# Spreading inverse softmax sums with a transpose and a constant selector

## The chip, the cores and the metric

The kernel runs on one core of a Trainium2 chip. The metric is the device time of one execution in microseconds (us); the time before is the median of three runs. TensorE is called PE here (PEld is its loading of weights), VectorE DVE, ScalarE ACT, GpSimd POOL, SyncE SP.

## The reference

Three layers follow each other, with batch 4, 8 heads, 576 tokens, head dimension 64:

```python
scores = scale * np.matmul(q, k.transpose(0, 1, 3, 2))
kth = np.partition(scores, -top_k, axis=-1)[..., -top_k:-top_k + 1]     # top_k = 32
scores = np.where(scores >= kth, scores, -1000000000.0)
attn = np.exp(scores - np.max(scores, axis=-1, keepdims=True))
attn = attn / (np.sum(attn, axis=-1, keepdims=True) + 1e-09)
out = np.matmul(attn, v)
...
x = sigmoid(xr @ w_r) * (np.maximum(xk @ w_k, 0) ** 2 @ w_v)            # xk, xr: token mixes of out
...
h = gelu(x @ w_in); u, v = halves of h; y = x + (u * (w_sg @ norm(v) + b_sg)) @ w_out
```

The change touches the division by the sum, and nothing else.

## The kernel before

The attention is worked off in 32 **units**: a batch, a pair of heads and a chunk of query tokens (`ch` 0 has 256 tokens, `ch` 1 has 320). In the first batch all chunks 0 come ahead of all chunks 1, later the two alternate. A unit is made of slots of 128 tokens (two for `ch` 0; two and a rest of 64 for `ch` 1, where both heads share the partitions). For each slot PE computes the scores (line 238), ACT copies them out of PSUM (240), DVE searches the 32nd largest score of each row by rounds of MAX8 (282) and MATCH_REPLACE8 (292) over the pairwise maxima and minima (273, 274), ACT takes the exponential (304), and DVE masks it and sums each row in one instruction (309). PE then transposes the masked rows (324, 327) and ACT copies them out (325, 328).

At the end of a unit `emit_unit` runs. DVE adds 1e-9 to the sums and inverts them (`rinv`, lines 345 and 346: 128 tokens on the partitions, 4 or 5 columns, one for each slot and head). PE multiplies the transposed probabilities by the values into the PSUM tile `px` (350, and 361 for the last 64 keys), with the head dimension on the partitions and the tokens along the free axis. The inverse sums have to stand in that layout too, so PE spreads each column of `rinv` over 64 partitions: the column, broadcast to 64 weights, times the identity (356, and 363 for the rest), both in full float32, into the PSUM tile `ps`. ACT copies `ps` to `rb` (366), and DVE multiplies `px` by `rb` into `x` (373, 377), from which the dense layers read.

PSUM has one double-bank for scores (tag `S`), three banks with the tag `tp` (the transposes of lines 198 to 216 and 324 to 336, and `px` and `ps`), and three with the tag `d` (dense layers). A `tp` bank is taken in the order in which the program asks for it and is free again when its last reader is done.

The dense layers of one batch (lines 522, 587, 607, 632, 713, 741) are put between the slots of the following attention work, by quotas of estimated PE time and by priorities; those of the last batch come after the last unit. A scheduler then sets the order of each engine's instructions from dependencies and priorities; on the chip each engine works its own list in that order.

Of the kernel before, what the change touches and what calls it, by code (L numbers as in the profile page):

```python
# [9 lines left out]
F32 = mybir.dt.float32  # L10
F32R = mybir.dt.float32r
I32 = mybir.dt.int32
U32 = mybir.dt.uint32
AF = mybir.ActivationFunctionType
OP = mybir.AluOpType
# [8 lines left out]
def computation(ctx, tc, dram, wscr, flag, fast, q, k, v, mu_k, mu_r, w_k, w_v, w_r, w_in, g_ln, w_sg, b_sg, w_out, out):  # L24
    nc = tc.nc
# [10 lines left out]
    const = ctx.enter_context(tc.tile_pool(name="const", bufs=1))  # L36
    sb = ctx.enter_context(tc.tile_pool(name="sb", bufs=1))
# [6 lines left out]
    ident = const.tile([128, 128], F32, name="ident")  # L44
# [5 lines left out]
    qrems = [const.tile([128, 2, 3, D], F32R, name=f"qrem{i}") for i in range(2)]  # L50
    for t in qrems:
        nc.vector.tensor_scalar(t[:, :, 1, :], ident[:, None, 0:64].to_broadcast([128, 2, D]), 0.0, None, op0=OP.mult)
    mu = const.tile([128, 2, KC], F32, name="mu")
    omu = const.tile([128, 2, KC], F32, name="omu")
    gln = const.tile([128, KC], F32, name="gln")
# [26 lines left out]
    def bank(tag, shape=(128, 512), dt=F32):  # L82
        if tag == "d" and rows[0] == NROWS:
            tag = ("d", "tp")[turn[0] % 2]
            turn[0] += 1
        return psum.tile(list(shape), dt, tag=tag, name=tag, bufs=BUFS[tag])
# [22 lines left out]
    for b in range(B):  # L109
# [4 lines left out]
        for p, chs in order:  # L114
            su = Rec()
            su.b, su.p, su.chs, su.raw, su.slots = b, p, chs, {}, []
            for ch in chs:
                u = Rec()
# [221 lines left out]
    def emit_unit(u):  # L340

        b, p, n, vr = u.su.b, u.su.p, u.n, u.su.raw["v"]
        nt = 4 if u.ch == 0 else 5
        rinv = sb.tile([128, 5], F32, tag="rinv", name="rinv", bufs=2)
        nc.vector.tensor_scalar(rinv[:, :nt], u.sums[:, :nt], 1e-9, None, op0=OP.add)
        nc.vector.reciprocal(rinv[:, :nt], rinv[:, :nt])
        px = bank("tp")
        for kc in range(4):
            for h in range(2):
                nc.tensor.matmul(px[64 * h:64 * h + 64, :n], lhsT=vr[:, 4 * h + kc, :], rhs=u.PT[h][:, kc, :n],  # L350
                                 start=(kc == 0), stop=False)

        ps = bank("tp")
        for i in range(2):
            for h in range(2):
                nc.tensor.matmul(ps[64 * h:64 * h + 64, 128 * i:128 * i + 128],
                                 lhsT=rinv[:, 2 * i + h:2 * i + h + 1].to_broadcast([128, 64]), rhs=ident,
                                 start=True, stop=True)
        for h in range(2):
            s = slice(64 * h, 64 * h + 64)  # L360
            nc.tensor.matmul(px[s, :n], lhsT=vr[s, 8, :], rhs=u.PTr[s, :n], start=False, stop=True)
            if u.ch:
                nc.tensor.matmul(ps[s, 256:320], lhsT=rinv[s, 4:5].to_broadcast([64, 64]), rhs=ident[s, s],
                                 start=True, stop=True)
        rb = sb.tile([128, 320], F32, tag="rb", name="rb", bufs=1)
        nc.scalar.activation(rb[:, :n], ps[:, :n], AF.Copy)
        if (b, p) not in xT:
            x = sb.tile([128, S + 1], F32, tag="x", name="x", bufs=5)
            xT[b, p] = x
            nc.gpsimd.memset(x[:, 0:1], 0.0)  # L370
        x = xT[b, p]
        o = 1 + 256 * u.ch
        nc.vector.tensor_tensor(x[:, o:o + 256].rearrange("p (i j) -> p j i", j=2),
                                px[:, :256].rearrange("p (j i) -> p j i", j=2),
                                rb[:, :256].rearrange("p (j i) -> p j i", j=2), op=OP.mult)
        if u.ch:
            nc.vector.tensor_tensor(x[:, 513:577], px[:, 256:320], rb[:, 256:320], op=OP.mult)
# [560 lines left out]
```

## Time and profile before

| | |
|---|---|
| median of 3 runs | 1001.48 us (998.19 to 1004.27) |
| profiled execution, its own time | 1001.01 us |
| its span, first to last instruction | 998.6 us |
| busy: PE, PEld | 878.3 us (88%), 762.9 us (76%) |
| busy: DVE, ACT, POOL | 836.4 us (84%), 695.6 us (70%), 529.9 us (53%) |
| mean granted clock of TensorE | 0.958 of full |
| first and last start of line 350, the values' product | 58.7 and 846.5 us |

The busy shares are means over the whole span. The attention fills the span from the start to about 849 us, and the last 150 us hold dense work of the last batches alone. So a share is read by stretch of time: which engine has no idle time there, and which engine's instructions make up the chain of waits there (the chain followed back from the last instruction, each step to what released it).

### The profile page before, as it was taken

The page shows a single profiled execution, that of the slowest core. Times are in us where ns is not written, and L with a number is a line of the kernel's source. Part 1 is how long each engine was busy: PE and PEld are TensorE (multiplying, and loading weights), DVE is VectorE, ACT ScalarE, POOL GpSimd, SP SyncE. Part 2 cuts the span into 40 slices and gives each one's busy share as a digit, 9 for nine tenths or more (in the row PEclk, how much of TensorE's full clock was granted, in tenths as well). Part 3 has the DMA queues.
Part 4 walks back from the last instruction along what each step waited for, and adds up shares of the span by engine and source line. Part 5 has one row for each costly group of instructions (what it writes and reads, how often), then busy time and mean ns, then how long its engine had stood idle before and what let it go on. Part 6 is the DMA issues. An engine that isn't in the chain of part 4 may idle for free.

```text
span 998.6 us, 18697 instructions
## 1 busy us (share of the span) xinstructions
PE 878.3 (88%) x6126; PEld 762.9 (76%) x6126; DVE 836.4 (84%) x2317; ACT 695.6 (70%) x1551; POOL 529.9 (53%) x626
## 2 busy tenths in 40 slices
PE   3465769889889999798999999999999998999997
PEld 2344548777778888677889979868999887899895
DVE  5899999998999999999999999999898765612142
ACT  5777878888887786677777679677775576554340
POOL 6688788775976168669243217598231145310051
PEclk9996779999999999998999999999999999999999
DMA  7954486888557645512333352363333436674441
GB/s 199 370 194 143 135 261 220 293 264 288 197 191 244 221 142 184 174 37 65 108 119 96 113 153 74 116 218 123 107 124 97 131 111 201 228 259 145 125 127 67
DMA packets 105067, 166.34 MB, mean 167 GB/s; under 512 B 19328, under 2 KB 74368, under 8 KB 104960
## 3 DMA queue, kind: packets, MB, share of 16 engines
q1 hardware_dynamic: 104960, 165.05, 50.7%
q8 instruction: 50, 0.82, 0.3%
q14 instruction: 57, 0.47, 0.1%
HBM read 134.27 MB, written 30.21 MB: 165 GB/s over the span
## 4 chain that ended last, share of the span: by engine, by line
DVE 37%; PE 37%; ACT 8%; DMA 7%; POOL 5%; issue 4%; SPq 1%; DVEq 0%; POOLq 0%; ACTq 0%
DVE M L282 11%; DVE T L292 8%; DVE E L309 8%; PE d L522 6%; PE d L587 6%; PE d L632 4%; DVE T L273 4%; DVE T L274 3%; PE d L713 3%; PE tp L522 3%; PE tp L350 2%; PE S L238 2%; PE d L741 2%; ACT E L304 2%; DMA w<-ws_k 1%
## 5 line engine op out<-in xcount | busy, mean ns | idle before, releaser
L282 DVE MAX8 M<-T 128x8 f32<-128x208 f32 (+3 forms) x576 | 260.5, 484 | 0.9
L292 DVE MATCH_REPLACE8 T<-M,T 128x208 f32<-128x208 f32 (+2 forms) x432 | 168.8, 393 | 0.0
L522 PE MATMUL d<-xm,w 128*128 128x288 f32 (+2 forms) x1008 | 161.1, 306 | 8.5 <-DMA w<-ws_k 4.1
L522 PEld LDWEIGHTS d<-xm,w 128*128 128x128 f32 x1008 | 141.1, 192 | 14.0 <-DMA w<-ws_k 4.9
L309 DVE SCALAR_TENSOR_TENSOR E<-S,M,E 128x576 f32<-128x576 f32 x144 | 145.2, 1035 | 0.8 <-ACT E L304 0.7
L238 PE MATMUL S<-kst,qst 128*128 128x288 f32 x512 | 110.5, 335 | 33.4 <-ACT S L240 16.9
L238 PEld LDWEIGHTS S<-kst,qst 128*128 128x128 f32 x512 | 83.2, 208 | 45.5 <-ACT S L240 22.5
L324 PE MATMUL tp<-ident,E 128*128 128x128 f32 x512 | 83.0, 291 | 28.9 <-ACT kst L207 14.7
L304 ACT ACTIVATE E<-S,nb 128x576 f32<-128x576 f32 x144 | 105.2, 774 | 0.8
L587 PE MATMUL d<-ksq,w 128*128 128x288 f32 (+2 forms) x672 | 104.7, 304 | 0.0
L240 ACT ACTIVATE S<-S 128x576 f32<-128x576 f32 x128 | 83.0, 648 | 29.9 <-DVE E L309 15.2
L587 PEld LDWEIGHTS d<-ksq,w 128*128 128x128 f32 x672 | 92.8, 191 | 0.9 <-issue 0.6
L324 PEld LDWEIGHTS tp<-ident,E 128*128 128x128 f32 x512 | 63.1, 148 | 37.6 <-ACT kst L207 15.4
L273 DVE TENSOR_TENSOR T<-S 128x576 f32<-128x576 f32 (+1 forms) x81 | 72.3, 892 | 21.7 <-ACT S L240 17.1
L350 PE MATMUL tp<-PT,rawv 128*64 128x256 f32 (+1 forms) x512 | 80.4, 442 | 8.2 <-ACT PT L325 8.2
L274 DVE TENSOR_TENSOR T<-S 128x576 f32<-128x576 f32 (+1 forms) x80 | 84.3, 1053 | 0.0
L325 ACT ACTIVATE PT<-tp 128x512 f32<-128x512 f32 x128 | 74.0, 599 | 3.3 <-PE tp L324 3.1
L350 PEld LDWEIGHTS tp<-PT,rawv 128*64 128x64 f32 x512 | 39.6, 147 | 36.2 <-ACT PT L325 9.4
L713 PE MATMUL d<-w,vn 128*128 128x288 f32 x392 | 61.0, 305 | 3.7 <-ACT u L674 2.7
L650 POOL TENSOR_SCALAR bag<-bag 128x1 f32<-128x1 f32 (+1 forms) x20 | 6.1, 304 | 108.0 <-DVE bag L649 106.7
L100 POOL TENSOR_TENSOR ksq<-tmp,ksq 128x576 fp32r<-128x576 f32 (+2 forms) x32 | 41.0, 1285 | 36.5 <-ACT ksq L98 35.0
L713 PEld LDWEIGHTS d<-w,vn 128*128 128x128 f32 x392 | 54.7, 191 | 5.5 <-ACT u L674 3.1
(165 smaller groups left out, 2009.1 us busy)
## 6 DMA issues: line engine op xcount, KB each, us to landing
w<-ws_k SPq DMA_DIRECT2D x40, 512.0 KB, 4.1
w<-ws_v SPq DMA_DIRECT2D x40, 512.0 KB, 4.0
w<-ws_sg SPq DMA_DIRECT2D x40, 288.0 KB, 3.4
w<-ws_r SPq DMA_DIRECT2D x20, 512.0 KB, 5.6
w<-ws_h SPq DMA_DIRECT2D x20, 512.0 KB, 3.7
w<-ws_u SPq DMA_DIRECT2D x20, 512.0 KB, 3.5
w<-ws_o SPq DMA_DIRECT2D x16, 512.0 KB, 4.8
rawk<-in_k_dram SPq DMA_DIRECT2D x40, 128.0 KB, 2.7
```

Source lines behind the costliest of these rows:

```text
L238: nc.tensor.matmul(ps[:, hf, :HALF], lhsT=su.qst[h, t.u.ch][:, a, 128 * t.i:128 * t.i + 128], rhs=su.kst[h][:, HALF * hf:HALF * hf + HALF] ...
L273: nc.vector.tensor_tensor(T[:, h, :HALF], t.S[:, h, :HALF], t.S[:, h, HALF:], op=OP.max)
L274: nc.vector.tensor_tensor(T[:, :, HALF:], t.S[:, :, :HALF], t.S[:, :, HALF:], op=OP.min)
L282: nc.vector.max(M[:, h, 8 * r:8 * r + 8], src[h][:, seg])
L292: mr = nc.vector.match_replace(L[h][:, seg], M[:, h, 8 * r:8 * r + 8], src[h][:, seg], NEG)
L304: nc.scalar.activation(t.E[:, h], t.S[:, h], AF.Exp, bias=nb[:, h:h + 1], scale=0.125)
L309: m = nc.vector.scalar_tensor_tensor(E, t.S[:, h], t.kv[h], E, op0=OP.is_ge, op1=OP.mult, accum_out=t.u.sums[:, 2 * t.i + h:2 * t.i + h + 1])
L324: nc.tensor.transpose(ps[:, kc, :], E[:, h, 64 * h + 128 * kc:64 * h + 128 * kc + 128], ident)
L350: nc.tensor.matmul(px[64 * h:64 * h + 64, :n], lhsT=vr[:, 4 * h + kc, :], rhs=u.PT[h][:, kc, :n], start=(kc == 0), stop=False)
L522: nc.tensor.matmul(ps[:, :n_], lhsT=w[:, bb, 128 * c:128 * c + 128], rhs=act[ch, which, c][:, a, o:o + n_], start=(c == 0 and i == 0), sto ...
L587: nc.tensor.matmul(ps[:, :nn], lhsT=w[:, bb, 128 * (f % 4):128 * (f % 4) + 128], rhs=kt[f][:, a, o:o + nn], start=(f == 0 and i == 0), sto ...
L713: nc.tensor.matmul(ps[:, :HALF], lhsT=act[b, "vn", i][:, a, 128 * m:128 * m + 128], rhs=W["sg", i, si][:, bb, :HALF], start=(j == 0), stop ...
```

## The change

DVE splits `rinv` into a rounded part and its remainder (`rhl`, ten columns: five and five; for `ch` 0 the fifth column of each is a copy of the fourth). PE transposes `rhl` once into ten rows of 128 columns, in the last quarter of the PSUM tile that `ps` was, and ACT copies them to `rT`. A constant selector `spread` of ten rows, built once on POOL, is then the weight: one product spreads two heads of one slot over all 128 partitions and adds rounded part and remainder, so there are two such products for each unit, and two more over 64 columns, with the selector `spreadr`, for the rest of `ch` 1. All of these are in the type float32r, in which one product shows as one record in the trace, where a product in full float32 shows as two (line 356: four instructions in a unit, eight records). The copy to `rb` and the multiplications into `x` stay as they were.

```diff
@@ -50,6 +50,15 @@
     qrems = [const.tile([128, 2, 3, D], F32R, name=f"qrem{i}") for i in range(2)]
     for t in qrems:
         nc.vector.tensor_scalar(t[:, :, 1, :], ident[:, None, 0:64].to_broadcast([128, 2, D]), 0.0, None, op0=OP.mult)
+    spread = const.tile([16, 4, 64], F32R, name="spread")
+    spreadr = const.tile([16, 2, 2, 64], F32R, name="spreadr")
+    nc.gpsimd.tensor_tensor(spread, ident[:16, 0:4, None].to_broadcast([16, 4, 64]),
+                            ident[:16, 5:9, None].to_broadcast([16, 4, 64]), op=OP.add)
+    nc.gpsimd.tensor_scalar(spreadr, ident[:16, None, None, 0:64].to_broadcast([16, 2, 2, 64]), 0.0, 1.0, op0=OP.mult,
+                            op1=OP.mult)
+    for h in range(2):
+        nc.gpsimd.tensor_tensor(spreadr[:, h, h], ident[:16, 4:5].to_broadcast([16, 64]),
+                                ident[:16, 9:10].to_broadcast([16, 64]), op=OP.add)
     mu = const.tile([128, 2, KC], F32, name="mu")
     omu = const.tile([128, 2, KC], F32, name="omu")
     gln = const.tile([128, KC], F32, name="gln")
@@ -342,26 +351,33 @@
         b, p, n, vr = u.su.b, u.su.p, u.n, u.su.raw["v"]
         nt = 4 if u.ch == 0 else 5
         rinv = sb.tile([128, 5], F32, tag="rinv", name="rinv", bufs=2)
+        rhl = sb.tile([128, 2, 5], F32R, tag="rhl", name="rhl", bufs=2)
+        rT = sb.tile([16, 128], F32R, tag="rT", name="rT", bufs=2)
         nc.vector.tensor_scalar(rinv[:, :nt], u.sums[:, :nt], 1e-9, None, op0=OP.add)
         nc.vector.reciprocal(rinv[:, :nt], rinv[:, :nt])
+        nc.vector.tensor_copy(rhl[:, 0, :nt], rinv[:, :nt])
+        nc.vector.tensor_tensor(rhl[:, 1, :nt], rinv[:, :nt], rhl[:, 0, :nt].bitcast(F32), op=OP.subtract)
+        if nt == 4:
+            nc.vector.tensor_copy(rhl[:, :, 4], rhl[:, :, 3])
+        pr = bank("tp", (128, 512), F32R)
+        ps = pr.bitcast(F32)
+        nc.tensor.transpose(pr[:10, 384:], rhl.rearrange("p a j -> p (a j)"), identr)
+        nc.scalar.activation(rT[:10], pr[:10, 384:], AF.Copy)
         px = bank("tp")
         for kc in range(4):
             for h in range(2):
                 nc.tensor.matmul(px[64 * h:64 * h + 64, :n], lhsT=vr[:, 4 * h + kc, :], rhs=u.PT[h][:, kc, :n],
                                  start=(kc == 0), stop=False)
-
-        ps = bank("tp")
-        for i in range(2):
-            for h in range(2):
-                nc.tensor.matmul(ps[64 * h:64 * h + 64, 128 * i:128 * i + 128],
-                                 lhsT=rinv[:, 2 * i + h:2 * i + h + 1].to_broadcast([128, 64]), rhs=ident,
-                                 start=True, stop=True)
         for h in range(2):
             s = slice(64 * h, 64 * h + 64)
             nc.tensor.matmul(px[s, :n], lhsT=vr[s, 8, :], rhs=u.PTr[s, :n], start=False, stop=True)
-            if u.ch:
-                nc.tensor.matmul(ps[s, 256:320], lhsT=rinv[s, 4:5].to_broadcast([64, 64]), rhs=ident[s, s],
-                                 start=True, stop=True)
+        for i in range(2):
+            nc.tensor.matmul(ps[:, 128 * i:128 * i + 128], lhsT=spread[:10, 2 * i:2 * i + 2].rearrange("r h d -> r (h d)"),
+                             rhs=rT[:10], start=True, stop=True)
+        if u.ch:
+            for h in range(2):
+                nc.tensor.matmul(ps[:, 256:320], lhsT=spreadr[:10, h].rearrange("r g d -> r (g d)"),
+                                 rhs=rT[:10, 64 * h:64 * h + 64], start=(h == 0), stop=(h == 1))
         rb = sb.tile([128, 320], F32, tag="rb", name="rb", bufs=1)
         nc.scalar.activation(rb[:, :n], ps[:, :n], AF.Copy)
         if (b, p) not in xT:
```

The PSUM tile is now asked for ahead of `px`, and the scheduler has set new orders on all engines. Three places follow. Names: `rinv`, `rhl`, `rT`, `spread` and `spreadr` are as above; `tp`, `d` and `S` are PSUM tiles; `T` and `M` belong to the search; `PT`, `PTr` are transposed probabilities; lines after the change are some 9 to 16 higher (364 is the transpose of `rhl`, 369 and 373 the values' products that were 350 and 361, 375 and 379 the new products, 333 the transposes of `E` that were 324, 207 those of `q` that were 198).

DVE, the first unit, from the inverse on. Before:

```order
L346 RECIPROCAL rinv<-rinv 128x4
L282 MAX M<-T_513 128x8 x2
L444 TENSOR_SCALAR d<-w 128x512
L292 MATCH_REPLACE T_513<-M,T_513 128x288 x2
L445 SCALAR_TENSOR_TENSOR w<-raw_437,d 128x512
L282 MAX M<-T_513 128x8 x2
```

After:

```order
L357 RECIPROCAL rinv<-rinv 128x4
L291 MAX M<-T_519 128x8 x2
L358 CAST rhl<-rinv 128x4
L460 TENSOR_SCALAR d<-w 128x512
L301 MATCH_REPLACE T_519<-M,T_519 128x288 x2
L359 TENSOR_TENSOR rhl<-rinv,rhl 128x4
L461 SCALAR_TENSOR_TENSOR w<-raw_443,d 128x512
L291 MAX M<-T_519 128x8 x2
L361 COPY rhl<-rhl 128x2
```

The three new instructions stand between pieces of the next slot's search, not behind each other.

PE, a unit of `ch` 1 in the second batch (at 395 to 399 us of the trace). Before:

```order
L350 MATMUL tp<-PT,rawv 64x320 x8
L356 MATMUL tp<-ident,rinv 64x128 x4
L361 MATMUL tp<-PTr,rawv 64x320
L363 MATMUL tp<-ident,rinv 64x64
L361 MATMUL tp<-PTr,rawv 64x320
L363 MATMUL tp<-ident,rinv 64x64
L198 MATMUL tp<-identr,splq 128x128 x4
L238 MATMUL S<-kst,qst 128x288 x4
```

After:

```order
L364 MATMUL tp<-identr,rhl 10x128
L729 MATMUL d<-w,vn 128x288 x6
L369 MATMUL tp<-PT,rawv 64x320 x8
L373 MATMUL tp<-PTr,rawv 64x320 x2
L207 MATMUL tp<-identr,splq 128x128 x4
L375 MATMUL tp<-rT,spread 128x128 x2
L379 MATMUL tp<-rT,spreadr 128x64 x2
L247 MATMUL S<-kst,qst 128x288 x4
```

The transpose has come to the front of the unit, with dense products behind it, and the new products stand behind the transposes of the next `q`, which wait for POOL.

PE, a unit of `ch` 0 in the last batch (at 762 to 767 us). Before:

```order
L350 MATMUL tp<-PT,rawv 64x256 x7
L356 MATMUL tp<-ident,rinv 64x128 x4
L607 MATMUL d<-ident,tmp 128x128 x2
L361 MATMUL tp<-PTr,rawv 64x256 x2
L607 MATMUL d<-ident,tmp 128x128 x2
L613 MATMUL d<-ident,tmp 64x128
L587 MATMUL d<-ksq,w 128x288 x12
L238 MATMUL S<-kst,qst 128x288 x4
```

After:

```order
L364 MATMUL tp<-identr,rhl 10x128
L369 MATMUL tp<-PT,rawv 64x256 x8
L373 MATMUL tp<-PTr,rawv 64x256 x2
L333 MATMUL tp<-ident,E_10634 128x128 x4
L623 MATMUL d<-ident,tmp 128x128 x2
L629 MATMUL d<-ident,tmp 64x128
L603 MATMUL d<-ksq,w 128x288 x3
L375 MATMUL tp<-rT,spread 128x128 x2
```

A transpose group of the next slot's `E` and dense work now lie between the values' products and the products with the selector, while the bank of the transposed sums is held.

## Rows read from the trace of the kernel before

**Rows 1.** Page, part 4: chain that ended last, by engine.

```profile
DVE 37%; PE 37%; ACT 8%; DMA 7%; POOL 5%; issue 4%; SPq 1%; DVEq 0%; POOLq 0%; ACTq 0%
```

**Rows 2.** Windows: PE, PEld, DVE, ACT, POOL busy us (x); PEclk; DMA share, GB/s.

```profile
50.00:150.00 100.00, 63.26 (x367) 46.79 (x368) 99.41 (x264) 79.65 (x191) 82.80 (x93) 0.78 0.57 184
150.00:300.00 150.00, 131.79 (x972) 113.70 (x971) 144.19 (x403) 127.11 (x303) 113.78 (x132) 0.95 0.71 242
300.00:550.00 250.00, 230.79 (x1675) 202.09 (x1674) 244.60 (x695) 186.52 (x417) 135.42 (x147) 0.96 0.43 139
...
700.00:850.00 150.00, 145.36 (x1057) 128.37 (x1056) 117.54 (x355) 98.31 (x210) 47.61 (x59) 0.99 0.41 131
```

**Rows 3.** Chain by line: 50-150, 150-300, 300-550, 550-700, 700-850 us.

```profile
by line: DVE M L282 19.2%; DVE T L292 14.6%; DVE E L309 13.8%; DVE T L273 8.2%; issue 8.1%; DVE w L445 6.3%; DVE T L274 5.7%; DMA w<-ws_r 5.0%; DVE d L444 3.9%; PE tp L350 3.7%; DMA rawsg<-in_moe_w_sg_dram 2.3%; PE d L522 1.5%; PE S L238 1.
by line: PE d L522 13.8%; DMA w<-ws_k 9.9%; DVE M L282 5.1%; DVE E L309 4.7%; PE d L632 4.3%; DMA ws_o<-w 3.8%; issue 3.3%; DVE T L292 3.3%; PE tp L350 3.1%; PE S L238 3.0%; PE d L587 2.9%; PE S L251 2.6%; PE tp L324 2.4%; ACT E L304 2.4%; 
by line: DVE M L282 27.3%; DVE T L292 18.1%; DVE E L309 17.7%; DVE T L274 8.2%; DVE T L273 7.8%; issue 5.1%; DMA ws_o<-w 2.3%; DMA raww<-in_moe_w_out_dram 2.0%; ACT E L304 1.4%; DVE x L373 1.4%; PE d L587 1.0%; DVE tmp L595 0.9%; DVE top L2
by line: PE d L632 9.5%; PE d L587 8.8%; POOL tmp L514 5.4%; issue 5.3%; PE d L713 5.2%; PE tp L350 4.3%; DVE M L282 4.1%; PE S L238 3.9%; POOL xm L100 3.9%; ACT E L304 3.8%; DVE T L292 3.6%; POOL tmp L513 2.8%; ACT L304 2.6%; POOL gt L100 
by line: PE d L587 17.3%; PE d L522 9.8%; PE d L632 7.5%; PE tp L350 6.3%; PE d L713 6.3%; DVE M L282 5.5%; PE S L238 5.0%; PE tp L324 3.8%; DVE E L309 3.8%; DVE T L292 3.6%; DVE T L274 2.5%; DVE T L273 2.2%; POOL tmp L653 2.2%; PE tp L361 
```

**Rows 4.** Windows of line 356 alone: PE busy us (x), PEld (x), clock, DMA.

```profile
150.00:300.00 150.00, 4.11 (x48) 3.28 (x48) 0.95 0.71 242
300.00:550.00 250.00, 7.16 (x80) 6.02 (x80) 0.96 0.43 139
550.00:700.00 150.00, 4.48 (x48) 3.56 (x48) 1.00 0.43 131
700.00:850.00 150.00, 5.00 (x48) 4.11 (x48) 0.99 0.41 131
```

**Rows 5.** Timeline of PE, 742 to 747 us: start, us, engine, line, instruction.

```profile
742.03 0.61 PE L356 MATMUL tp<-ident,rinv 128*64 128x128 f32 x8
742.57 0.76 PE L361 MATMUL tp<-PTr,rawv 64*64 64x320 f32 x4
743.16 0.29 PE L363 MATMUL tp<-ident,rinv 64*64 64x64 f32 x4
743.37 2.80 PE L587 MATMUL d<-ksq,w 128*128 128x288 f32 x19
746.01 0.46 PE L198 MATMUL tp<-identr,splq 128*128 128x128 f32 x4
746.31 0.51 PE L206 MATMUL tp<-identr,splk 128*128 128x128 f32 x4
```

**Rows 6.** Timeline of DVE, 47 to 49 us.

```profile
47.51 0.15 DVE L345 TENSOR_SCALAR rinv<-sums 128x4 f32<-128x4 f32 x1
47.57 0.08 DVE L292 MATCH_VALUE_LOAD T<-M,T 128x8 f32 x1
...
48.40 0.16 DVE L346 RECIPROCAL rinv<-rinv 128x4 f32<-128x4 f32 x1
48.48 0.78 DVE L282 MAX8 M<-T 128x8 f32<-128x288 f32 x2
```

**Rows 7.** Groups by line: two ACT copies (busy us, mean ns).

```profile
L325 ACT ACTIVATE PT<-tp 128x512 f32<-128x512 f32 x128 | 74.0, 599 | 3.3 <-PE tp L324 3.1
...
L328 ACT ACTIVATE PTr<-tp 128x128 f32<-128x128 f32 x64 | 18.0, 282 | 3.2 <-PE tp L327 3.1
```

**Rows 8.** Timeline of POOL at the start.

```profile
3.38 0.72 POOL L100 TENSOR_TENSOR splk<-rawk,splk 128x256 fp32r<-128x256 f32 x1 [1.88 <-ACT splk L98]
```

**Rows 9.** Waits of PE: who waited, for what, us, times, longest.

```profile
PE tp L198 <- POOL splq L173: 8.3, 6, 4.0
...
PE tp L324 <- ACT rb L366: 3.2, 4, 1.3
```

**Rows 10.** Line 350: duration ns min/median/max, first and last start us.

```profile
L350 PE MATMUL tp<-PT,rawv x512: 378/432/691, 58.7 to 846.5; 128*64 128x256 f32 x86, 128*64 128x320 f32 x85
```

## Prediction, made before the changed kernel ran

> **What bounds the kernel now.** The chain of waits by engine [rows 1] comes first: DVE and PE carry 37% of it each, ACT 8%. So neither a dearer DVE nor a cheaper PE counts in full, and the stretches decide. The busy times by stretch [rows 2] show DVE without idle time from 50 to 150 us (99.41 of 100) and from 300 to 550 us (244.60 of 250), while from 700 to 850 us it has slack (117.54 of 150) and PE has little (145.36). Before 50 us the first loads lead, and behind 850 us stands dense work that the change does not touch. The chain by line [rows 3] says the same by names: adding the lines of each stretch that are shown, DVE has 72%, 13%, 81%, 8% and 18% of the five stretches, PE about 6%, 32%, 1%, 32% and 56%. The reader is to see there that the change gives PE time where DVE leads and takes DVE time everywhere.
>
> Line 356 has eight records for each unit, so its counts from 150 us on [rows 4] place 6, 10, 6 and 6 of the 32 units in the last four stretches, and the other 4 in the first. The order in which the units come makes 4, 1, 5, 3 and 3 of these `ch` 0 and 0, 5, 5, 3 and 3 `ch` 1.
>
> **What PE loses and gains.** In a unit near 742 us the eight records of line 356 fill 742.03 to 742.57, that is 0.54 us, and line 363 adds 743.16 to 743.37, 0.21 us [rows 5]. Removed: 32 x 0.54 + 16 x 0.21 = 20.6 us. Added are one transpose and two products over 128 columns, and two over 64 for `ch` 1. The nearest row is line 198, four such transposes in float32r in 0.30 us (746.01 to 746.31), 0.075 each [rows 5]. I take that for all, also for 64 columns: 32 x 3 x 0.075 + 16 x 2 x 0.075 = 9.6 us. PE is relieved of 11.0 us: 0.315 in a unit of `ch` 0, 0.375 in one of `ch` 1. The bounds for a new PE instruction are 0.05 (line 363: 0.21 for four records) and 0.135 (line 356: 0.54 for four instructions, if the new ones cost as much); the relief lies between 14.2 and 3.3 us. On the path it counts by PE's share of the stretch: 1.26 x 0.06 + 2.19 x 0.32 + 3.45 x 0.01 + 2.07 x 0.32 + 2.07 x 0.56 = 2.6 us.
>
> **What DVE gains.** A unit gets a rounding copy and a subtraction, one of `ch` 0 a third copy: 80 instructions of ten columns at most, 12, 13, 25, 15 and 15 by stretch. Their like are lines 345 and 346, which show as 0.15 and 0.16 us, but the next instruction starts 0.06 and 0.08 us after them [rows 6]. In the new order nearly all stand between pieces of the search, as these two do, so I take 0.08 each, 6.4 us in all; the bounds are 0.06 and, should each hold its successor to its end, 0.16. Where DVE has no idle time I count them in full, 37 x 0.08 = 3.0 us; elsewhere by DVE's share, (13 x 0.13 + 15 x 0.08 + 15 x 0.18) x 0.08 = 0.4 us. Together 3.4 us, between 2.6 and 6.8.
>
> The Trainium skill, "VectorE: DVE Perf Modes", section "The DRAIN you can't avoid", says that the next DVE instruction does not start until the pipe is empty, and advises few instructions, which speaks against this change. By that the 80 would cost their whole 0.15 to 0.16 us, and the path would gain some 3 us over what I sum here. The trace does not bear it out for instructions that follow each other without need of each other's result: 0.06 and 0.08 us are what it shows [rows 6].
>
> **What ACT gains.** 32 copies of ten partitions by 128 columns. The nearest row is line 328, 128 columns, 0.282 us with its overlap [rows 7]; I take 0.2 (bounds 0.1 and 0.28), 6.4 us in all, and at ACT's 8% of the chain [rows 1] 0.5 us. The copy to `rb` is unchanged.
>
> **What stands elsewhere.** Four small POOL instructions build the selectors at the start. POOL is idle there for 1.88 us before the first split of `k` [rows 8], which takes 0.72 us for 256 columns on 128 partitions; two of 256 columns at that price and two of 64 at less just fit, so I cost them at nothing, at most 0.5 us if the split is late. No DMA is added or taken away, and no queue is passed. The new waits are two. PE's transpose waits for DVE, and behind it in PE's order stand the values' products; in the new order the last DVE piece stands six instructions of the search behind the inverse, of which the first two took 0.78 us [rows 6]. In the first unit of the trace the values' products began at 58.7 us [rows 10], 10.3 us after the inverse at 48.40 [rows 6], so there the wait is hidden; where a unit has less room, it shows. The products with the selector wait for ACT's `rT`, and `rb` and `x` behind them; in the new order all of the values' products stand between the transpose and them, and cover that. I cost both at nothing here, and take them up as a rival.
>
> **Sum.** 1001.0 (the profiled execution's own time) + 3.4 + 0.5 - 2.6 = 1002.3. That execution is 0.5 us under the median of the runs, so the median should be 1002.8: no difference that a measurement of this kernel can tell, for which I take 0.5%, or 5 us.
>
> **Rival 1, slower: the bank and the place in PE's queue.** The transposed sums now hold one of the three `tp` banks from ahead of the values' products until `rb` is copied, and `px` holds another. In 13 of the 32 units the new order puts a transpose of the next `E` between the transpose of the sums and the products with the selector, and in 8 it puts the transposes of `q` there. These have one bank left, so one group waits until ACT has emptied the group before. For it speak waits that are there already: `E` for `rb` 3.2 us, `q` for POOL's split 8.3 us [rows 9]; the second now delays `rb` too. Against it: there is dense work between, which PE can do meanwhile, and in 300 to 550 us a PE wait of that size ends ahead of DVE. The price is one copy of a transposed group, 0.6 us [rows 7], in each of the 18 units of the three stretches where PE carries a good share: 10.8 us, so 1013.6. It decides from 0.2 us of wait in each of these 18 units on: 3.6 us, which with the 1.3 of the sum make 5.
>
> **Rival 2, faster: PE is the bound throughout.** If DVE's full stretches are full because instructions wait inside them for scores that PE delivers late, the whole relief counts: 1002.8 + 2.6 - 11.0 = 994.4. For it speaks that PE is busy for 231 of 250 us in the stretch where DVE leads [rows 2]. Against it: the chain there names PE with 1% [rows 3].
>
> **Rival 3, no relief.** The new products could cost as much as the old ones, one for one. Then 11.0 becomes 3.3, the path loses 0.8 instead of 2.6 us, and the time is 1004.6, still within 0.5%. Nothing in the trace speaks for it: line 198 shows the price of float32r.
>
> **How the numbers follow.** The forecast has a chance of 0.38 and rival 3 one of 0.10, both within 0.5%: 0.48. Rival 1 gets 0.30, since a new order on all engines meets a kernel in which both leaders have little idle time, and a late bank costs more than the small terms of the sum. Rival 2 gets 0.22. The range goes to 994.0 below and 1014.0 above, so that the prices of rivals 1 and 2 lie in it; it leaves out a full PE relief at the lower bound of the instruction price, and bank waits in more than the 18 units.
>
> **What would show it.** In the profile after, the new products and the transpose should take under 0.1 us each from start to start, the DVE pieces 0.06 to 0.09 us, and the last start of the values' product, at 846.5 us before [rows 10], should have moved by less than 5 us, with the tail behind it unchanged in length. DVE should stay over 97% busy from 300 to 550 us. Rival 1 would show as longer waits of `E` and `q` transposes for `rb` and `x`, and of the products with the selector for `rT`; rival 2 as a last unit some 8 us earlier. I am wrong if the last unit moves by more than 5 us while the small instructions cost what I say: then the order decided, not the prices.

## The result, and the profile after

The changed kernel took 1016.06 us (median of 4 runs, 1015.54 to 1016.79), the kernel before 1001.04 us beside it: a ratio of 1.0144, with a 95% interval of 1.0114 to 1.0174. It is slower by 15 us. The forecast was 1002.8 us, no difference; the range ended at 1014.0, so the result lies outside it.

The page of the changed kernel, busy time by engine and then the chain that ended last, by engine:

```profile
span 1015.0 us, 18408 instructions
...
PE 879.0 (87%) x5934; PEld 753.8 (74%) x5934; DVE 860.9 (85%) x2397; ACT 704.6 (69%) x1587; POOL 529.7 (52%) x630
...
DVE 40%; PE 34%; ACT 10%; DMA 5%; issue 4%; POOL 4%; SPq 1%; DVEq 0%; POOLq 0%; ACTq 0%
```

DVE is busy for 24.5 us more than before (836.4 us there), with 80 more instructions. PE is busy as long as before (878.3), with 192 records fewer. DVE's share of the chain has risen from 37% to 40%, and PE's has fallen from 37% to 34% [rows 1]. By stretch (columns as in [rows 2]):

```profile
50.00:150.00 100.00, 58.05 (x322) 41.41 (x323) 99.58 (x265) 75.45 (x183) 78.69 (x87) 0.80 0.53 174
150.00:300.00 150.00, 126.67 (x881) 106.61 (x880) 143.82 (x391) 123.40 (x295) 106.80 (x131) 0.94 0.67 225
300.00:550.00 250.00, 228.53 (x1553) 195.78 (x1553) 243.18 (x705) 185.40 (x426) 136.06 (x147) 0.94 0.45 145
700.00:850.00 150.00, 146.14 (x1060) 128.97 (x1060) 135.75 (x404) 104.81 (x233) 57.48 (x69) 1.00 0.35 112
```

DVE is as full as before where it led, and has more to do; and between 700 and 850 us, where it had slack, it now has 135.75 us of work instead of 117.54. The delay grows with the units. The inverse of the first one starts at 48.7 us (48.40 before, [rows 6]), and later ones, counted in the same order, at 155.4 against 150.3, 271.8 against 262.0, 424.9 against 410.2 and 524.3 against 505.6; the last one starts at 854.5 against 835.7. The last value product starts here:

```profile
L369 PE MATMUL tp<-PT,rawv x512: 379/432/741, 59.4 to 863.3; 128*64 128x256 f32 x86, 128*64 128x320 f32 x85
```

That is 16.8 us later than before [rows 10]; the tail behind it has kept its length.

The groups by line show what the new instructions cost (busy us, mean ns, idle time ahead of them):

```profile
L359 DVE TENSOR_TENSOR rhl<-rinv,rhl 128x4 fp32r<-128x4 f32 (+1 forms) x32 | 10.3, 322 | 0.1
L358 DVE CAST rhl<-rinv 128x4 fp32r<-128x4 f32 (+1 forms) x32 | 9.8, 306 | 0.1
L361 DVE CAST rhl<-rhl 128x2 fp32r<-128x2 f32 x16 | 4.7, 295 | 0.0
L357 DVE RECIPROCAL rinv<-rinv 128x4 f32<-128x4 f32 (+1 forms) x32 | 5.4, 169 | 0.0
...
L375 PE MATMUL tp<-rT,spread 10*128 10x128 f32 x64 | 13.9, 296 | 0.0
L375 PEld LDWEIGHTS tp<-rT,spread 10*128 10x128 f32 x64 | 9.4, 183 | 7.4 <-issue 5.5 <-ACT E L313 0.7 <-ACT PT L334 0.4
L364 PE MATMUL tp<-identr,rhl 128*10 128x128 f32 x32 | 7.7, 240 | 10.8 <-DVE rhl L361 3.6 <-ACT PT L343 3.3 <-ACT PT L334 2.9
L379 PE MATMUL tp<-rT,spreadr 10*128 10x64 f32 x32 | 5.6, 256 | 0.0
```

The reader is to see that the split's instructions (358, 359, 361) have about twice the mean of the RECIPROCAL beside them, on tiles of the same size. Means include the overlap with the next instruction. Counted along the timeline from each start to the next start, or to the end where that is earlier, the three lines hold DVE for 7.3, 8.0 and 3.8 us, 19.1 us in all or 0.24 us each; the forecast had 0.08. Their durations are not spread evenly (min/median/max ns behind the count):

```profile
L358 DVE CAST rhl<-rinv x32: 142/214/790, 49.4 to 854.8; 128x4 fp32r<-128x4 f32 x16, 128x5 fp32r<-128x5 f32 x16
```

```profile
L359 DVE TENSOR_TENSOR rhl<-rinv,rhl x32: 139/160/1116, 51.1 to 855.0; 128x4 fp32r<-128x4 f32 x16, 128x5 fp32r<-128x5 f32 x16
```

Here is the longest one in the timeline of the changed kernel, first DVE, then POOL (GpSimd):

```profile
157.42 1.12 DVE L359 TENSOR_TENSOR rhl<-rinv,rhl 128x5 fp32r<-128x5 f32 x1
158.46 1.35 DVE L282 TENSOR_TENSOR T<-S 128x576 f32<-128x576 f32 x1
```

```profile
157.21 1.30 POOL L463 TENSOR_TENSOR w<-w 128x512 int32<-128x512 int32 x1
```

The subtraction of five columns starts while POOL works on a tile of 512, and ends at 158.54, 0.03 us after POOL does (157.21 + 1.30 = 158.51). Another one of the same line, where POOL is idle ahead of 551.70:

```profile
551.23 0.14 DVE L359 TENSOR_TENSOR rhl<-rinv,rhl 128x5 fp32r<-128x5 f32 x1
551.30 0.74 DVE L291 MAX8 M<-T 128x8 f32<-128x576 f32 x1
```

```profile
551.70 0.74 POOL L109 TENSOR_TENSOR splk<-rawk,splk 128x256 fp32r<-128x256 f32 x1 [4.25 <-ACT splk L107]
```

It takes 0.14 us, and the next instruction starts 0.07 us after its start. Of the 80 instructions, 34 start with no POOL instruction running: none of these takes more than 173 ns. The other 46 start beside one; 35 of them take over 230 ns, and each of these 35 ends 10 to 30 ns after a POOL instruction that ran at its start. Not every POOL instruction delays them: two of the other eleven start beside a power of a single column (line 667, 554 ns in the median), take 142 and 143 ns, and end before it does. The RECIPROCAL of line 357 starts beside POOL 17 times, and takes 157 to 178 ns there. The sign stood in the trace of before, in a line that the prediction read in one place only [rows 6]. This is that line in the view by source there:

```profile
L345 DVE TENSOR_SCALAR rinv<-sums x32: 141/149/1421, 47.5 to 835.5; 128x4 f32<-128x4 f32 x16, 128x5 f32<-128x5 f32 x16
```

The addition of 1e-9, too, takes 149 ns in the median and up to 1421. Ten of the 32 take over 180 ns, and all ten end 22 to 29 ns after a POOL instruction.

The Trainium skill, "SBUF — State Buffer", section "Who interferes with whom", states such a rule: VectorE copies, casts and operations with a scalar in a two-port mode, and operations with two inputs in SBUF against a GpSimd instruction that reads SBUF, share a port pair with GpSimd as an exclusive lock, and the one that comes second waits for the whole instruction of the other. The 35 ends agree with it, and so does the RECIPROCAL, which is not among these forms. Which ports an instruction used, and in which mode it ran, no trace here shows.

On PE, lines 356 and 363 had held it for 24.6 us (start to next start, as above). The new lines hold it for 4.8 (364, 0.15 each), 10.3 (375, 0.16 each) and 4.5 us (379, 0.14 each), together 19.6. So PE is relieved of 5.0 us, not 11.0. An old product of line 356 held PE for 0.16 us as well (20.9 us for 128).

### The profile page after: what moved, and what is told of

Its sections match the earlier page's. It is cut to its first block, busy times and chain, and to the rows that moved or that the text cites. A ratio compares the mean times of both kernels' runs of the same rounds, so it can differ in the third digit from the quotient of the medians.

```text
span 1015.0 us, 18408 instructions
## 1 busy us (share of the span) xinstructions
PE 879.0 (87%) x5934; PEld 753.8 (74%) x5934; DVE 860.9 (85%) x2397; ACT 704.6 (69%) x1587; POOL 529.7 (52%) x630
## 4 chain that ended last, share of the span: by engine, by line
DVE 40%; PE 34%; ACT 10%; DMA 5%; issue 4%; POOL 4%; SPq 1%; DVEq 0%; POOLq 0%; ACTq 0%
DVE M L291 11%; DVE E L318 9%; DVE T L301 8%; PE d L603 6%; PE d L648 5%; PE d L729 4%; DVE T L282 4%; DVE T L283 3%; PE tp L369 3%; PE d L757 2%; PE S L247 2%; PE tp L538 2%; PE d L538 2%; ACT E L313 2%; PE tp L333 2%
## 5 line engine op out<-in xcount | busy, mean ns | idle before, releaser
L318 DVE SCALAR_TENSOR_TENSOR E<-S,M,E 128x576 f32<-128x576 f32 x144 | 153.6, 1094 | 1.1 <-ACT E L313 1.1
L333 PE MATMUL tp<-ident,E 128*128 128x128 f32 x512 | 85.1, 292 | 34.8 <-ACT kst L216 23.9
L603 PE MATMUL d<-ksq,w 128*128 128x288 f32 (+2 forms) x672 | 108.9, 309 | 1.0 <-DMA w<-ws_v 0.7
L603 PEld LDWEIGHTS d<-ksq,w 128*128 128x128 f32 x672 | 95.3, 195 | 3.5 <-DMA w<-ws_v 1.0
L282 DVE TENSOR_TENSOR T<-S 128x576 f32<-128x576 f32 (+1 forms) x81 | 70.0, 864 | 15.3 <-ACT S L249 12.0
L283 DVE TENSOR_TENSOR T<-S 128x576 f32<-128x576 f32 (+1 forms) x80 | 80.3, 1004 | 0.0
L369 PEld LDWEIGHTS tp<-PT,rawv 128*64 128x64 f32 x512 | 37.3, 149 | 31.3 <-issue 8.5
L109 POOL TENSOR_TENSOR splk<-rawk,splk 128x256 fp32r<-128x256 f32 x40 | 34.8, 871 | 44.7 <-ACT splk L107 44.4
```

Source lines behind the costliest of these rows:

```text
L282: nc.vector.tensor_tensor(T[:, h, :HALF], t.S[:, h, :HALF], t.S[:, h, HALF:], op=OP.max)
L283: nc.vector.tensor_tensor(T[:, :, HALF:], t.S[:, :, :HALF], t.S[:, :, HALF:], op=OP.min)
L318: m = nc.vector.scalar_tensor_tensor(E, t.S[:, h], t.kv[h], E, op0=OP.is_ge, op1=OP.mult, accum_out=t.u.sums[:, 2 * t.i + h:2 * t.i + h + 1])
L333: nc.tensor.transpose(ps[:, kc, :], E[:, h, 64 * h + 128 * kc:64 * h + 128 * kc + 128], ident)
L603: nc.tensor.matmul(ps[:, :nn], lhsT=w[:, bb, 128 * (f % 4):128 * (f % 4) + 128], rhs=kt[f][:, a, o:o + nn], start=(f == 0 and i == 0), sto ...
```

## The experiments

**Theory A:** the 80 VectorE instructions are the loss, because their forms wait for the GpSimd instruction that is running, and VectorE's time is on the path. **Theory B:** the loss comes from elsewhere, from the bank and the place of the transpose in PE's queue (rival 1 of the prediction) or from the new order of the work. Later theories stand with their runs.

### Taking one part in or out

**The split alone, in the kernel before** (its result is read by nobody):

```diff
         nc.vector.reciprocal(rinv[:, :nt], rinv[:, :nt])
+        rhl = sb.tile([128, 2, 5], F32R, tag="rhl", name="rhl", bufs=2)
+        nc.vector.tensor_copy(rhl[:, 0, :nt], rinv[:, :nt])
+        nc.vector.tensor_tensor(rhl[:, 1, :nt], rinv[:, :nt], rhl[:, 0, :nt].bitcast(F32), op=OP.subtract)
+        if nt == 4:
+            nc.vector.tensor_copy(rhl[:, :, 4], rhl[:, :, 3])
```

> The kernel before, with the three DVE instructions of the split added (80 in all) and their result read by nothing; PE, the banks and ACT do what they did. Theory A (the new DVE instructions each wait for the POOL instruction that runs, 0.24 us on the mean, on a DVE without idle time): 1012 to 1020 us, the new instructions again at a mean of 0.2 us or more from start to next start. Rival B (the bank held longer and the place in PE's order): these are absent, so only the 3.4 us of the forecast, 1001 to 1006 us.

Measured: 1037.68 us, ratio 1.0372 (1.0342 to 1.0402). The direction is A's, but the loss of 36 us is nearly twice the upper end of what A expected.

**The same with RECIPROCALs:**

```diff
-        nc.vector.tensor_copy(rhl[:, 0, :nt], rinv[:, :nt])
+        nc.vector.reciprocal(rhl[:, 0, :nt], rinv[:, :nt])
...
```

> As the run with the split alone, but the 80 added DVE instructions are reciprocals of the same shapes, whose result is read by nothing. In the trace after, the reciprocal never took over 0.19 us whatever POOL did. Theory A: 0.06 to 0.1 us each, 5 to 7 us in all, 1003 to 1008 us. Rival C (any small instruction costs 0.24 us there): 1012 to 1020 us, as the split. Rival B: 1001 to 1006 us.

Measured: 1014.26 us, ratio 1.0122 (1.0091 to 1.0153). The two differ by 23 us, and even RECIPROCALs cost 12.7 us, more than A expected for them; that lies in the range of rival C, though they hold VectorE for 0.10 each and not for its 0.24. Neither theory covers both runs, and they differ in more than the form: the schedule is made anew for each kernel, and without the 80, VectorE's sequence in the two traces is the same for its first 134 instructions only. So the order had to be held, below.

**The change with the split on ACT and GpSimd:**

```diff
-        nc.vector.tensor_copy(rhl[:, 0, :nt], rinv[:, :nt])
-        nc.vector.tensor_tensor(rhl[:, 1, :nt], rinv[:, :nt], rhl[:, 0, :nt].bitcast(F32), op=OP.subtract)
+        nc.scalar.activation(rhl[:, 0, :nt], rinv[:, :nt], AF.Copy)
+        nc.gpsimd.tensor_tensor(rhl[:, 1, :nt], rinv[:, :nt], rhl[:, 0, :nt].bitcast(F32), op=OP.subtract)
...
```

> The change, with the rounding copy and the copy of the fifth column on ACT and the subtraction on POOL; DVE has nothing new, PE's work and the bank are those of the change. Theory A: DVE gets back most of its 19 us, 997 to 1004 us. Rival B: still 1010 to 1018 us.

Measured: 1003.67 us, ratio 1.0009 (0.9978 to 1.0040). The transpose, the bank, the copy and the products are those of the change, and the 15 us are gone, as A has it. But the schedule is new here too (the traces show another order of PE), so rival 1 is decided only by the runs in the changed kernel's own order, below.

**The change without a split,** the inverse transposed in float32, a selector of four or five rows:

```diff
-        pr = bank("tp", (128, 512), F32R)
-        nc.tensor.transpose(pr[:10, 384:], rhl.rearrange("p a j -> p (a j)"), identr)
+        ps = bank("tp")
+        nc.tensor.transpose(ps[:nt, 384:], rinv[:, :nt], ident)
...
```

> The change without a split: the inverse sums are transposed in float32 as they are, and a float32 selector of five rows spreads them, in two records a product. No new DVE instruction; the transpose, the copy to rT and the bank's longer hold stay. Theory A: 996 to 1003 us. Rival B: 1010 to 1018 us.

Measured: 1010.83 us, ratio 1.0086 (1.0053 to 1.0120), outside A's range and in B's, though VectorE has none of the 80. The groups by line show what else is different in this run:

```profile
L368 PE MATMUL tp<-rT,spread 4*128 4x128 f32 (+1 forms) x128 | 22.6, 296 | 0.4 <-ACT rT L358 0.4
...
L357 PE MATMUL tp<-ident,rinv 128*4 128x128 f32 (+1 forms) x32 | 9.4, 293 | 0.4 <-ACT PT L333 0.3
L372 PE MATMUL tp<-rT,spreadr 5*128 5x64 f32 x64 | 8.9, 258 | 0.0
```

In float32 the products have twice the records (128 and 64 for 64 and 32). From start to next start the three lines hold PE for 31.5 us, 7 more than the lines removed. So the run exchanges the price of the split for one on PE, in an order of its own, and does not separate the two; whether these 7 us make its loss of 9 us is not shown.

### The order held

In the next runs each instruction is tied to the one ahead of it on its engine, without a semaphore, in the order of another kernel's schedule. The traces of the runs with all engines tied show that order on PE, VectorE, ACT and GpSimd, apart from the instructions put in, taken out or replaced.

```diff
     computation(pools, tc, dram, wscr, flag, True, *args)
+    pin(tc)
...
+        for a, b in itertools.pairwise(order):
+            tc.add_manual_dep(engines[e][b], engines[e][a].name, how, reason="order of the other kernel")
```

**The changed kernel's order, RECIPROCALs for the split:**

```diff
-        nc.vector.tensor_copy(rhl[:, 0, :nt], rinv[:, :nt])
+            nc.vector.reciprocal(rhl[:, 0, :nt], rinv[:, :nt])
...
```

> The changed kernel with every engine's order kept exactly as it is in the changed kernel (each instruction is tied to the one ahead of it on its engine), and the 80 instructions of the split replaced one for one by RECIPROCALs of the same tiles, so only the form of the VectorE instructions differs. The hi and lo parts are not computed: the output is not the reference's. Theory A (the COPY and the subtraction each wait for the GpSimd instruction that is then running, a RECIPROCAL does not): the 80 cost 0.10 us each as in the run with reciprocals, 8 us instead of the 19.1 us of the changed kernel, and the time falls by 8 to 13 us, to 1003-1008. Theory B (the split's form costs nothing much; the changed kernel is late because its schedule has another order of work): the order is the same, so the time stays within 4 us of the changed kernel, 1012-1018.

Measured: 1005.01 us, ratio 1.0043 (1.0022 to 1.0064). Only the form differs from the changed kernel, with the transpose in the same place in PE's queue and the banks held alike, and 11.05 us go. That is Theory A's number; B's is excluded. The new lines:

```profile
L360 DVE RECIPROCAL rhl<-rhl 128x4 fp32r<-128x4 f32 (+1 forms) x32 | 5.4, 170 | 0.1
...
L359 DVE RECIPROCAL rhl<-rinv 128x4 fp32r<-128x4 f32 (+1 forms) x32 | 5.2, 163 | 0.1
...
L362 DVE RECIPROCAL rhl<-rhl 128x2 fp32r<-128x2 f32 x16 | 2.3, 146 | 0.0
```

From start to next start they hold VectorE for 8.3 us instead of 19.1, 0.10 us each.

**The old order, with the split put in behind each inverse,** as in the first diff of this section:

> The kernel before with every engine's order kept exactly as it is there, and only the 80 VectorE instructions of the split put in behind each inverse, their result read by nobody. PE, ACT, GpSimd and the DMA queue have the same instructions in the same order as before. Theory A: 80 instructions of 0.24 us, and the longer waits of the other forms that wait for GpSimd, on the path: 1015-1026. Theory B (most of the 36 us that the same insertion cost with a free schedule was the new order): 1004-1010.

Measured: 1028.99 us, ratio 1.0279 (1.0247 to 1.0311). B is excluded, and A's range is passed by 3 us: directly behind each other, and behind the inverse whose result they read, the 80 hold VectorE for 26.4 us here, 0.33 each.

**The old order, with RECIPROCALs put in:**

> The same as the run with the split in the old order, but with 80 RECIPROCALs in the place of the split's instructions. Theory A: 80 x 0.10 us, of which half to all is on the path: 1005-1010, and at least 8 us under the run with the split in the old order. Theory B: within 4 us of that run. If it stays under 1004, the 12.7 us that reciprocals cost with a free schedule were nearly all the order of the work.

Measured: 1014.72 us, ratio 1.0130 (1.0099 to 1.0162). The form is worth 14.3 us in this order, as A has it. But the number alone costs 13.8 us, more than A expected. The timeline of VectorE in the same unit of the two runs, first the split, then the RECIPROCALs:

```profile
102.30 0.17 DVE L346 RECIPROCAL rinv<-rinv 128x4 f32<-128x4 f32 x1
102.50 0.40 DVE L348 CAST rhl<-rinv 128x4 fp32r<-128x4 f32 x1
102.93 1.18 DVE L349 TENSOR_TENSOR rhl<-rinv,rhl 128x4 fp32r<-128x4 f32 x1
104.15 0.55 DVE L351 CAST rhl<-rhl 128x2 fp32r<-128x2 f32 x1
```

```profile
101.30 0.16 DVE L346 RECIPROCAL rinv<-rinv 128x4 f32<-128x4 f32 x1
101.49 0.18 DVE L348 RECIPROCAL rhl<-rinv 128x4 f32<-128x4 f32 x1
101.71 0.18 DVE L349 RECIPROCAL rhl<-rhl 128x4 f32<-128x4 f32 x1
101.92 0.17 DVE L351 RECIPROCAL rhl<-rhl 128x2 f32<-128x2 f32 x1
102.00 0.80 DVE L282 MAX8 M<-T 128x8 f32<-128x288 f32 x2
```

Each reads the result of the one ahead, and starts 0.19 to 0.22 us after it; the MAX8, which needs none of them, starts 0.08 us after the last. So a small instruction has three prices here: 0.06 to 0.08 us between instructions that don't need it, about 0.2 us in a chain, and the rest of a GpSimd instruction on top where its form waits. The new lines and the inverse, which now has a reader directly behind it, add 14.3 us of VectorE time, and the mask of line 309 4.0 us; in all VectorE was busy for 16.6 us more, idle for 1.6 us less, and the kernel took 13.8 us more. In the run with the split it was busy for 31.3 us more, and its last instruction ended 31.5 us later; by the medians the kernel took 28.0 us more. In the fixed order nearly all of VectorE's added time reaches the end.

**The old order without the addition of 1e-9:**

```diff
-        nc.vector.tensor_scalar(rinv[:, :nt], u.sums[:, :nt], 1e-9, None, op0=OP.add)
-        nc.vector.reciprocal(rinv[:, :nt], rinv[:, :nt])
+        nc.vector.reciprocal(rinv[:, :nt], u.sums[:, :nt])
```

> The kernel before in its own order on every engine, without the addition of 1e-9 to the sums (32 VectorE instructions, 8.9 us in the trace of before, mean 277 ns against a median of 149): the reciprocal reads the sums directly. The sums are at least 1 in float32, where adding 1e-9 changes no bit. Theory A (this instruction, too, waits for GpSimd, and VectorE's time is on the path): 3 to 9 us less than before, 992-998. Theory B (such small instructions lie beside other waits): 999-1003.

Measured: 996.04 us, ratio 0.9947 (0.9925 to 0.9968), less than both kernels. The line held VectorE for 6.1 us from start to next start, and 4.9 us of it are gained. That is in A's range.

### The rest of the change

**The changed kernel's order without the split,** the inverse written as fp32r and its remainder left out:

```diff
-        nc.vector.tensor_copy(rhl[:, 0, :nt], rinv[:, :nt])
...
+            nc.vector.reciprocal(rhl[:, :nt], rinv[:, :nt])
...
+        nc.tensor.transpose(pr[:nt, 384:], rhl[:, :nt], identr)
```

> The PE part of the change alone, in the changed kernel's order on every engine: the 80 VectorE instructions of the split are left out, the RECIPROCAL writes the inverse as fp32r, and the transpose and the two products work on these four or five rows. The lo part of the inverse is left out. Theory A (VectorE's 80 instructions are the whole loss, and the transpose, its copy and the products beside them cost nothing): the run with reciprocals in this order was at 1005.0 with 8.2 us of VectorE time in the 80, so 996-999. Theory B (the longer way from the inverse over the transpose, the copy and the products to x costs something by itself): 1001-1005.

Measured: 1000.22 us, ratio 0.9994 (0.9976 to 1.0011), between the two ranges. Against the changed kernel, in the same order, 15.8 us go, which is the whole loss; so rival 1, whose bank and place in PE's queue are still there, falls as its cause. What is left of the change, with its order, neither gains nor loses more than the interval allows, some 2 us.

**The same without the addition of 1e-9:**

```diff
-        nc.vector.tensor_scalar(rinv[:, :nt], u.sums[:, :nt], 1e-9, None, op0=OP.add)
...
+            nc.vector.reciprocal(rhl[:, :nt], u.sums[:, :nt])
```

> As the run without the split, and without the addition of 1e-9 to the sums as well (sums of at least 1, where it changes no bit): the RECIPROCAL reads the sums. Theory A: the addition holds VectorE for 6 to 8 us in this order and its removal gave 4.9 us in the old order, so 4 to 8 us under the run without the split: 989-995, less than both kernels. Theory B (PE, at 88%, sets the time by now): within 2 us of the run without the split.

Measured: 993.89 us, ratio 0.9925 (0.9900 to 0.9951). The lowest median of all, 6.3 us under the run with the addition, as A has it; its interval overlaps that of the old order without the addition (0.9925 to 0.9968). The page has VectorE at the same busy time as the old order without the addition (831.1 us), and PE 5.9 us lower (875.8 there):

```profile
PE 869.9 (88%) x5934; PEld 748.2 (76%) x5934; DVE 831.1 (84%) x2285; ACT 702.5 (71%) x1587; POOL 533.8 (54%) x630
```

**The same kernel with a free schedule** (no call of `pin`):

> The same kernel with no order tied down, so that the schedule is made anew. If the order of the work is worth little: within 3 us of the kernel with the tied order. The free schedules so far moved the time by 1 us (reciprocals, 1014.3 free against 1014.7 tied) and 8.7 us (split, 1037.7 free against 1029.0 tied), so 986-1004 is possible.

Measured: 1002.90 us, ratio 1.0020 (1.0006 to 1.0035). The order alone is worth 9 us, more than the 3 us of the first expectation.

**The same kernel with VectorE, GpSimd and the DMA queue in the old order,** PE and ACT free:

> The same kernel as the one without split and addition, with VectorE, GpSimd and the DMA queue in the old order (that of the kernel before) and PE and ACT free. VectorE has exactly the instructions of the old-order kernel without the addition (996.0), so the difference from that one is what the transpose, the copy and the selector products do in the place of the spread products. Theory A with the prediction's PE term (about 2.6 us of PE's relief on the path): 992-995. Theory B (PE's relief lies beside VectorE's work and nothing is gained): 995-998. Theory C (the longer way to x makes VectorE wait at the products of x, 32 of up to 0.3 us): 999-1006.

Measured: 1012.22 us, ratio 1.0115 (1.0087 to 1.0143). That is above all three ranges. The waits of VectorE (who for what, us, times, longest), first of the fastest kernel, then of this one:

```profile
DVE tmp L605 <- PE d L597: 14.9, 5, 4.0
...
DVE x L383 <- ACT rb L376: 8.5, 6, 4.3
```

```profile
DVE tmp L605 <- PE d L597: 25.8, 9, 5.4
DVE x L383 <- ACT rb L376: 23.1, 14, 4.3
```

Apart from the order the two programs are the same. The product of `x` waits for ACT's copy `rb` 14 times instead of 6, and a product of the dense part waits longer as well. In the old-order kernel without the addition, whose VectorE has the same order as here, the product of `x` waits 5 times, 8.2 us in all. That is theory C's sign, though its number was too small: the way from the sums to `x` now runs over the transpose, ACT's `rT`, the selector's products and `rb`, and an order of VectorE that was made for the shorter way may leave no room for it. How much of the 16 us over the old-order kernel without the addition is that, and how much PE's and ACT's new order, stays open: an old order held on all engines with the change in it was not run.

## Why the prediction was wrong

**The step that failed** is "I take 0.08 each, 6.4 us in all" for DVE's 80 instructions, with the upper bound of 0.16 and the count on the path of 3.4 us. Measured: 19.1 us held, 0.24 each, and 15.8 us on the path (the changed kernel less the same order without the split). Of these, 11.05 us are the form (the wait for GpSimd) and the other 4.8 us the number, together with the rows of the remainder in the products, which the run without the split leaves out too. Taken from the ratios, each run against the kernel before beside it, the three are 15.0, 10.1 and 4.9 us; each is known to some 3 us. The like chosen was right for one of the two lines and wrong for the other: the RECIPROCAL of line 346 does not wait, the addition of line 345 does, and [rows 6] caught it in one of its short cases. The bound was taken from these same two rows, so the range was too short above. The price alone does not lead out of the range: at 0.24 each, the shares of the prediction give 10.2 us on the path and a time of 1009.6. The share on the path failed with it.

**The share on the path.** I discounted DVE's time outside its full stretches to 8%, 13% and 18% of the chain. The runs with the order held show little of that discount: in the changed order 15.8 us arrive of the 18.1 us by which VectorE's busy time differs (in the trace of the run without the split, its slowest execution), and in the old one 28.0 of 31.3 and 13.8 of 16.6 us. The shares also did not stay what they were. This is the chain of the changed kernel by line, from 150 to 300 us and from 700 to 850 us:

```profile
by line: DVE M L291 13.2%; DVE E L318 10.6%; DVE T L301 9.7%; DVE T L283 6.2%; issue 6.0%; DVE T L282 4.4%; ACT E L313 3.7%; PE d L648 3.5%; DMA rawk<-in_k_dram 3.4%; DVE w L461 3.3%; PE tp L369 2.5%; PE d L603 2.5%; ACT PT L334 2.3%; PE tp
by line: DVE M L291 14.1%; PE d L603 12.9%; DVE T L301 10.5%; DVE E L318 10.1%; PE d L648 7.5%; DVE T L282 5.7%; issue 4.2%; DVE T L283 3.5%; PE tp L369 2.8%; PE tp L333 2.6%; POOL tmp L669 2.2%; PE S L247 2.1%; POOL vn L109 1.7%; ACT S L24
```

The shown lines of DVE add up to 47% and 44%, where the prediction read 13% and 18% before [rows 3]. From 150 to 300 us that is the new order: the run without the split, in the same order, shows 46% there. From 700 to 850 us it is the split: that run shows PE's lines ahead there, and none of DVE. So a share of the chain before the change was not what DVE's added time would count by after it. (The sums of [rows 3] are also somewhat low, since the view is cut off at its end.) That the delay is handed on from unit to unit, because each unit's inverse, masks and search stand in one line on DVE, fits the starts of the inverses above, 18.7 us late at 524 us and 18.9 at the last.

**PE's relief** was 5.0 us, not 11.0. What was removed had held PE for 24.6 us, not 20.6; what was added holds it for 19.6, not 9.6. The transposes in float32r that gave 0.075 us [rows 5] have weights of 128 rows and 128 columns, with an LDWEIGHTS of 140 ns in the median; the weights of the new products have ten rows and 128 columns and take 183 ns. The new instructions come at 0.14 to 0.16 us, above my bound of 0.135. Why is not shown: the transpose of the sums, at 0.15, has an LDWEIGHTS of 85 ns only. It made little difference: without the split the rest of the change measured 0.9994 (0.9976 to 1.0011), and a net gain of 2.1 us for PE and ACT was forecast.

**Rivals 2 and 3.** PE is not the bound throughout: VectorE's added time reached the end while PE's instructions stayed the same (the split in the old order). Rival 3 was right on PE: the new products cost what the old ones cost, one for one (0.16 us each), and its relief of 3.3 us is nearer to the measured 5.0 than the forecast's 11.0. Its time of 1004.6 was missed for the same reason as the forecast's, the term of DVE.

**ACT's copies** took 250 ns each, where I took 0.2 us, within the bounds of 0.1 and 0.28.

**The waits.** PE's transpose waited 10.8 us in all, of which DVE's last piece ended 4.7 us. Rival 1's number (1013.6) is near the result by luck, for its cause was not the loss: the order of PE and the banks are unchanged in the runs at 1005.01 and 1000.22 us. Its kin, a later `rb`, shows in one run, where the old order of VectorE was forced on the change.

**The rule of the DRAIN.** The prediction weighed the Trainium skill, "VectorE: DVE Perf Modes", section "The DRAIN you can't avoid", against [rows 6] and followed the rows. The same section goes on to say that a next instruction that is not held starts earlier, which the prediction left out, and the advice of few instructions stands under "Rules for kernel authors" on that page; so the section does not speak against 0.06 and 0.08 us. The chains of the old-order runs agree with the rule where each instruction reads the one ahead (0.19 to 0.22 us); between independent ones the rows still show 0.06 to 0.08. In the changed kernel's order the RECIPROCALs in the places of the 80 cost 0.10 each.

**The test I set** was "I am wrong if the last unit moves by more than 5 us while the small instructions cost what I say". It moved by 16.8 us, and they did not cost that. DVE over 97% busy from 300 to 550 us came true (243.18 of 250).

**Order.** The mask of line 309 (318 now) costs 8.5 us more than before in the changed kernel, and the search's preparation in lines 273 and 274 (282 and 283) 6.2 us less. Both stand in the run without the split as well (+9.1 and -9.4), so they are not the split's; that they belong to the new order fits, and they cancel in large part.

## What to carry to other kernels

Take the price of a small instruction on VectorE from the minimum, median and maximum of its line, never from one place in the timeline; where the maximum is ten times the median, look at what GpSimd does in that moment, and look for a form that doesn't wait, or another engine. Where one engine is full over most of the span, reckon with nearly all of its added time, as here, whatever its share of the chain. And where a scheduler makes the order, hold the order before comparing: here the order alone moved one and the same kernel by 9 us.

## What was not expected of the hardware

A copy or subtraction of four or five columns that takes 0.15 us takes up to 1.12 us beside a GpSimd instruction, and ends 10 to 30 ns after it. A weight load of ten rows by 128 columns took 183 ns, against 141 ns (median) for one of 128 rows by 128 columns (line 207) and 85 ns for one of 128 rows by ten columns in the same kernel; the products with these few rows were no cheaper on PE. Leaving out one addition on 128 by 4 elements in each of 32 units, which changes no bit, gave 0.5% of the whole kernel (0.9947, 0.9925 to 0.9968).
